# Turned probability blocks through DRAM: one write and four reads a part, in place of 16 SBUF-to-SBUF moves

## The chip, the cores and the metric

The kernel runs on one core of one Trainium2 chip. The metric is the device time of one execution in microseconds (us); the kernel before has a median of 1175.51 us over three runs.

## The reference

The inputs are `q`, `k`, `v` of shape (8, 8, 576, 64): 8 batches, 8 heads, 576 positions, 64 channels a head. All is float32.

```
q_rot, k_rot = rotate(q), rotate(k)                 # rotary embedding, per position
scores = q_rot @ k_rot^T / sqrt(64)                 # 576 x 576 for each head
attn   = exp(scores - rowmax); attn /= (rowsum + 1e-9)
x      = concat of heads of (attn @ v)              # (8, 576, 512)
x_prev = x shifted by one position, zeros first
xk, xr = mu * x + (1 - mu) * x_prev                 # two mixes, mu_k and mu_r
k = relu(xk @ w_k); v = (k * k) @ w_v               # 512 -> 1024 -> 512
out = sigmoid(xr @ w_r) * v
```

So an attention stage feeds, batch by batch, a channel mix of three matrix products.

## The kernel before, in words

**Units of work.** Heads are taken in pairs: 8 batches of 4 pairs, 32 pairs. For one pair the queries are cut into nine blocks of 128 query columns, written here as units u = 0 to 8: four from each head and a shared last one. For each unit TensorE (PE) makes 128 x 576 scores (line 417), VectorE (DVE) takes the negated row maximum `nm` (line 428), and ScalarE (ACT) writes the exponentials `pe` with their row sums (line 438). The product with `v` needs the probabilities with keys on the partitions, so they must be turned.

**Two ways of turning.** The first four pairs (`EARLY = 4`) are turned by PE through an identity matrix (`plan_turn`, line 463). The other 28 pairs are turned in two steps. First, DVE transposes 32 x 32 blocks within each group of 32 partitions (line 443) and writes them into a tile `p`, one tile for each of two parts g = 0, 1 of a pair, `[128, 18, 128]` and `[128, 18, 160]` float32. Afterwards `p` holds, on partition group a (32 partitions) and block b (one of 18 blocks of 32 keys), a block that belongs on another group of partitions. Second, `plan_move` moves it into `rows_t[g]`, `[128, 4, 5, 128 or 160]`, in which keys stand on partitions. The 18 key blocks are cut into four strips of 5, 5, 4 and 4 blocks (`STRIPS`), one for each group of 32 target partitions. One DMA takes source group a and strip s to target group s: 4 x 4 = 16 DMAs a part (lines 502 to 510), each of 32 rows. Then 20 matmuls a part make `av` (line 529), DVE multiplies by the reciprocal row sums `rb` (lines 536 and 541), and the result `xT` goes to the channel mix.

**Reciprocal sums.** For each pair, DVE inverts the sums (lines 479 to 482), one DMA writes them to a DRAM tile `inv` (line 486) and two read them back, broadcast, into `rb` (line 492). This is a way through DRAM that the kernel already has.

**Channel mix.** For each half batch (288 positions) the mixes `mxf` are split into a rounded high part and a low remainder (`mxh`, `mxl`), and each product is three matmuls of 288 columns (lines 609, 610, 611). Its weights come as 64-bit words, 20 blocks of 128 x 512, through one `raw` buffer (line 291), and DVE, ACT and POOL turn each into float32 high and low parts.

**Buffers.** One tile of each of `p` part 0, `p` part 1, `rows_t[0]`, `rows_t[1]`, one `values` tile (line 386), two tiles for loaded and rotated q and k (`nat`, line 340), one `rb`, one `raw`.

**What sets the order.** The order of instructions on every engine is written out in advance by a planner (`Plan.issue`, line 109). Each operation has a rank, a cost and its predecessors; in the planner's own model of time, an engine that comes free takes the ready operation of the lowest rank. Ranks are a pair's or half batch's start time plus offsets from the tables `R`, `EARLY_R`, `PB` and `MB` (lines 30 to 42); the `B_` numbers bias the choice of engine where there are two. All DMAs are issued by SyncE (SP). In the planner a DMA is an operation of SP with a cost of 350 ns, and then one of a single modelled DMA engine, at 360 bytes a ns, for the moves 190. On the chip each engine executes its list in that order: an SP entry whose semaphore has not come holds all entries behind it.

The changed steps stand in `dma` (line 104), and in `plan_move` (line 472), whose results `d["M", g]` the product in `plan_values` (line 543) waits for.

Of the kernel before, what the change touches and what calls it, by code (L numbers as in the profile page):

```python
# [14 lines left out]
F32 = mybir.dt.float32  # L15
# [7 lines left out]
P = 128  # L23
# [3 lines left out]
WG = (128, 160)  # L27
STRIPS = ((0, 5), (5, 5), (10, 4), (14, 4))
EARLY = 4
R = dict(k=-179.52, q=-112.39, v=-377.25, cs=587.95, mu=696.88, ld=1946.21, rope0=636.06, rope1=1296.91,  # L30
         rope2=-189.65, split0=1185.84, split1=-372.65, u0=-519.54, u1=-378.68, u2=-113.17, u3=-312.32, u4=-344.5,
         mx=-450.29, ex=-554.02, tp=586.99, dm=61.24, da=46.42, dw=-1222.76, dr2=1374.29, av=766.79, ah=73.72,
         nr=5.44, ev=-725.53, m0=154.44, mh=0.64, mk=-102.03, mr=350.75, ms=170.57, mx1=-292.97, mx2=291.49,
         mx3=-1004.93, mg=24.03, mv=17.23, dr=-272.53, key0=-863.9, key1=938.21, key2=405.18, gate0=982.35,
         gate1=-652.3, wk0=-13.84, wk1=-71.85, wr0=-294.97, wr1=132.08, wv0=-65.2, wv1=95.49)
EARLY_R = dict(k=-367.76, q=-526.32, v=-276.86, ld=-806.66, rope0=-55.23, rope1=221.54, rope2=308.84,
               split0=-128.56, split1=747.9, u0=-654.44, u1=-336.85, u2=-413.68, u3=-209.13, u4=-92.85, mx=99.4,
               ex=-456.12, tp=-58.57, dm=-427.42, da=-338.79, dw=-832.67, dr2=171.88, av=-196.14, ah=417.64,
               nr=184.01, ev=-1013.41)
PB = (-1117.66, -32.72, -757.09, -55.52, 346.01, 25.88, -122.08, -92.28)  # L40
B_COPY, B_ROPE, B_SPLIT, B_LOW, B_MIX, B_SQUARE, B_RELU = -881.07, 63.63, 520.96, 1365.24, 1028.59, -1244.85, -157.99
MB = (-73.1, -357.44, 21.16, -309.47, 391.67, -92.21, 254.91, 283.5)
CY = 12
BUFS = dict(nat=2, kh=2, kl=1, qh=2, ql=1, vs=1, pe=4, pe3=8, p0=1, p1=1, s=2, s3=3, nm=6, sums=2, rb=1, pt0=1, pt1=1, t=2, xT=5, raw=1, we=1, wm=1, mxf=2, mxh=5, mxl=5, acc=2, hr=2, kkh=8, kkl=8, rt=3)

# [5 lines left out]
def act(n):  # L51
    return 0.833 * n + 100


def dve(n):
    return 1.04 * n + 70


def dve2(n):
    return 0.52 * n + 75  # L60
# [12 lines left out]
class Plan:  # L73
# [16 lines left out]
    def op(self, engine, rank, cost, fn, after=(), uses=()):  # L90


        o = len(self.ops)
        if isinstance(engine, str):
            engine, fn = {engine: (cost, 0, engine == "G")}, lambda e, fn=fn: fn()
        opens = [s for s in uses if s.opener is None]
        for s in uses:
            s.users += 1
        for s in opens:
            s.opener = o  # L100
        self.ops.append((engine, rank, None, fn, tuple(after), tuple(uses), opens))
        return o

    def dma(self, rank, nbytes, fn, after=(), uses=(), rate=360):

        o = self.op("S", rank, 350, fn, after, uses)
        return self.op("D", rank, nbytes / rate, lambda: None, [o], uses)

    def issue(self):
# [92 lines left out]
def rope_attention_channel_mix(ctx, tc, qt, kt, v, cs, mu, w_k, w_v, w_r, out):  # L202
# [3 lines left out]
    nc = tc.nc  # L206
    B, NP, _, _, S = kt.shape
# [9 lines left out]
    dram = ctx.enter_context(tc.tile_pool(name="dram", bufs=1, space=bass.MemoryType.DRAM))  # L217
# [22 lines left out]
    def one(n, bias=0.0):  # L240

        return {"A": (act(n) + 30, 0, False), "V": (dve2(n), bias, True)}
# [6 lines left out]
    V, A, G, T = nc.vector, nc.scalar, nc.gpsimd, nc.tensor  # L249
    plan = Plan(BUFS)  # L250
    op, dma, Slot = plan.op, plan.dma, plan.slot

    def combine(e, out, a, b, op):
# [22 lines left out]
    rows_t = [const.tile([P, 4, 5, n], F32, name=f"rows_{n}") for n in WG]  # L276
# [55 lines left out]
    def plan_rope(t, d, n, src, have, plain, load_rank):  # L332
# [22 lines left out]
        def turned(which, i, t):  # L355
# [3 lines left out]
            return [o, op(two(P, B_ROPE), t, 0, lambda e: turn_last(e, which, i), [ld] + have, [slot])]  # L359

        ld = dma(load_rank, P * 8 * w, load, [], [slot])
        ms = turned("s", 1, t + d["r"]["rope0"])
        mc = turned("c", 0, t + d["r"]["rope1"])
# [11 lines left out]
    def plan_prep(t, b, g):  # L375
        d = live[b, g]
        d["r"] = EARLY_R if PAIRS.index((b, g)) < EARLY else R
        d["bg"], d["plain"] = (b, g), PAIRS.index((b, g)) < PLAIN
        first = PAIRS[0] == (b, g)
        plan_rope(t + d["r"]["k"], d, "k", kt[b, g], tables["cs"], d["plain"], -339.0 if first else t + d["r"]["k"] + d["r"]["ld"])  # L380
        plan_rope(t + d["r"]["q"], d, "q", qt[b, g], tables["cs"], d["plain"], -289.0 if first else t + d["r"]["q"] + d["r"]["ld"])
        sv = d["sv"] = Slot("vs")

        def load_v():
            d["vf"] = values_t[sv.index % BUFS["vs"]]
            nc.sync.dma_start(d["vf"], v[b, g])

        d["v"] = dma(t + d["r"]["v"] + d["r"]["ld"], P * 4 * 10 * D, load_v, [], [sv])
# [83 lines left out]
    def plan_move(t, d):  # L472


        ss, sr = d["ss"], Slot("rb")
        w = {}

        def inverse():
            V.tensor_scalar_add(d["sums"][:, 0:9], d["sums"][:, 0:9], 1e-9)
            V.reciprocal(d["sums"][:, 0:9], d["sums"][:, 0:9])  # L480
            V.tensor_copy(d["sums"][:, 9:10], d["sums"][:, 4:5])
            V.transpose(d["sums"], d["sums"])

        def write():
            w["dram"] = dram.tile([4, 32, 32], F32, tag="inv", name="inv", bufs=4)
            nc.sync.dma_start(w["dram"].rearrange("a u n -> (a u) n"), d["sums"])

        def read(x):
            if "rb" not in d:
                d["rb"] = sb.tile([P, 4, 160], F32, tag="rb", name="rb", bufs=BUFS["rb"])  # L490
            src = w["dram"][:, 5 * x:5 * x + 5, :].rearrange("a u n -> a (u n)").unsqueeze(0).to_broadcast([D, 4, 160])
            nc.sync.dma_start(d["rb"][(up, dn)[x]], src)

        o = op("V", t + d["r"]["nr"], 500, inverse, [d["E", u] for u in range(9)], [ss])
        o = dma(t + d["r"]["dw"], P * 128, write, [o], [ss])
        d["R"] = [dma(t + d["r"]["dr2"] + 0.1 * x, D * 4 * 640, lambda x=x: read(x), [o], [sr]) for x in range(2)]
        d["sr"] = sr

        if d["early"]:
            return  # L500

        def move(g, a, s):
            at, n = STRIPS[s]
            nc.sync.dma_start(rows_t[g][32 * s:32 * s + 32, a, 0:n, :], d["p", g][32 * a:32 * a + 32, at:at + n, :])  # L504

        for g, cs in enumerate(GROUPS):
            ready = [d["T", u] for c in cs for u in ((4,) if c == 4 else (c, c + 5))]
            for a in range(4):
                for s in range(4):
                    d["M", g].append(dma(t + d["r"]["dm"] + d["r"]["da"] * g + 0.01 * (4 * a + s), 32 * STRIPS[s][1] * 4 * WG[g], lambda g=g, a=a, s=s: move(g, a, s), ready, [d["sp", g], d["spt", g]], rate=190))  # L510

    N0 = S // 2

    def plan_values(t, d):
# [4 lines left out]
        for g in range(2):  # L519
# [18 lines left out]
            def divided_last(x):  # L538
                r = (up, dn)[x]
                acc = w[1][:, 0:384].rearrange("p (a n) -> p a n", a=4)[r, :, 80 - 80 * x:96 - 80 * x]  # L540
                V.tensor_tensor(out=d["x"][r, 513:S + 1].rearrange("p (a n) -> p a n", n=16), in0=acc, in1=d["rb"][r, :, 128 + 16 * x:144 + 16 * x], op=ALU.mult)

            o = op("T", t + d["r"]["av"] + d["r"]["ah"] * g, 2350 + 540 * g, products, d["M", g] + [d["v"]], [s_a, d["sv"], d["spt", g]])
            e[g] = [op("V", t + d["r"]["ev"] + d["r"]["ah"] * g, dve(256) + 30, divided, [o] + d["R"], [s_a, sx, d["sr"]])]
            if g:
                e[g] += [op("V", t + d["r"]["ev"] + d["r"]["ah"] * g + 0.1 * x, dve(64) + 30, lambda x=x: divided_last(x), [o] + d["R"], [s_a, sx, d["sr"]]) for x in range(2)]
        z = op("G", t + d["r"]["ev"], 110, lambda: G.memset(d["x"][:, 0:1], 0.0), [], [sx])
        d["X", 0], d["X", 1] = e[0] + e[1] + [z], e[0] + e[1]

    def plan_attention():  # L550
        for pi, bg in enumerate(PAIRS):
            plan.group = 2 * pi
            d, t = live[bg], PT * pi + (PB[pi] if pi < len(PB) else 0)
            plan_prep(t, *bg)
# [4 lines left out]
            for c in range(5):  # L559
                plan.group = 2 * pi + 0.1 * c  # L560
                plan_unit(t + (EARLY_R if pi < EARLY else R)[f"u{c}"], d, c)
            plan.group = 2 * pi
# [7 lines left out]
    def plan_mix(t, b, half, which, f, hold):  # L570
# [24 lines left out]
        o = op({"A": (act(n) + 130, 0, False), "V": (dve2(n) + 60, B_MIX, True)}, t, 0, previous, d["X", half] + [rest], [sx, s_f])  # L595
        o = op({"V": (dve(n) + 60, 0, True)}, t + R["mx1"], 0, mixed, [o], [sx, s_f])
        h = op(one(n, B_SPLIT), t + R["mx2"], 0, high, [o], [s_f, s_h])
# [102 lines left out]
    for b in range(B):  # L700
        plan_channel_mix(b, 4 * PT * b + R["m0"] + MB[b], 4 * PT * (b + 1) + R["m0"] + MB[b])
    with tc.manual_schedule():
# [65 lines left out]
```

## Time and profile before

| | |
|---|---|
| runs | 1166.67, 1175.51, 1175.69 us; median 1175.51 |
| profiled execution | 1166.59 us, of which the profile's span is 1164.8 us |
| PE busy | 981.5 us, 84% |
| DVE busy | 822.4 us, 71% |
| ACT, POOL busy | 532.7 us, 488.5 us |
| DMA | 157.49 MB in 95,425 packets; the SP queue's packets took 49.1% of 16 engines' span |
| HBM | 71.90 MB read, 9.96 MB written |
| PE's granted clock, mean | 0.939 of full speed |

The page first gives the busy time of each engine, then the span in slices, the DMA queues, the chain of work that ended last (followed back from the last instruction), and the costliest groups of instructions. "SPq" is SyncE issuing a DMA; "L504" is line 504. A busy share is an average over stages, so the stages are looked at by themselves in what follows: a start (to about 125 us) with the early pairs and the first weights, a stage to about 250 us in which the moves have begun and the last weights are still being made, a long even stage to about 1060 us, and a tail of channel mix alone.

### The profile page before, as it was taken

Reading aid. Unit: us, or ns where it says so; the run is one execution under the profiler, and the core shown is the slowest. Engines: PE = TensorE matmul, PEld = TensorE weight load, DVE = VectorE, ACT = ScalarE, POOL = GpSimd, SP = SyncE. Lnnn points to the kernel's source line nnn. Section 1 sums busy time; section 2 is a strip of 40 time slices with the busy share of each in tenths; the row PEclk is TensorE's granted clock in tenths of the full one; section 3 lists DMA queues with packets and bytes.
Section 4 is the critical chain, followed back from the end, with each engine's and each line's share of the span. In section 5 each row is a group of like instructions: output and inputs, shape, how many; then the busy total and the mean of one; then the engine's idle time right before and its main releaser. Section 6 shows DMA issues by size and latency. Waiting matters only on the chain.

```text
span 1164.8 us, 19561 instructions
## 1 busy us (share of the span) xinstructions
PE 981.5 (84%) x6866; PEld 791.3 (68%) x6866; DVE 822.4 (71%) x1465; ACT 532.7 (46%) x1317; POOL 488.5 (42%) x495
## 2 busy tenths in 40 slices
PE   2687688678887978999999989998988888988898
PEld 1444355466676767787778767776867776776788
DVE  6989987855775666776877777796767876663442
ACT  2556445423455344554565444555445543432133
POOL 4545357612155354436564435445445524311111
PEclk9999778579897999999999999998999998999999
DMA  5434576415564355556656556655455555443000
GB/s 171 146 120 164 160 199 176 128 51 140 138 168 113 102 150 161 137 141 182 169 155 162 152 132 192 173 152 145 140 138 158 143 135 153 119 106 79 16 22 21
DMA packets 95425, 157.49 MB, mean 135 GB/s; under 512 B 23008, under 2 KB 47584, under 8 KB 95328
## 3 DMA queue, kind: packets, MB, share of 16 engines
q1 hardware_dynamic: 95328, 156.25, 49.1%
q8 instruction: 54, 0.88, 0.3%
q14 instruction: 43, 0.35, 0.1%
HBM read 71.90 MB, written 9.96 MB: 70 GB/s over the span
## 4 chain that ended last, share of the span: by engine, by line
PE 37%; SPq 19%; DVE 18%; DMA 14%; issue 5%; POOL 3%; ACT 3%; DVEq 0%; POOLq 0%; ACTq 0%
SPq L504 17%; PE scores L609 9%; PE av L529 8%; PE scores L611 7%; PE scores L610 7%; PE scores L417 5%; DVE nm L428 4%; DMA rows<-p 4%; DVE p L443 3%; DMA xq<-in_qt 3%; DMA xk<-in_kt 2%; DMA values<-in_v 2%; DMA out_dram<-rt 1%; POOL xq L254 1%; DVE mxf L585 1%
## 5 line engine op out<-in xcount | busy, mean ns | idle before, releaser
L438 ACT ACTIVATE pe<-scores,nm 128x576 f32<-128x576 f32 x252 | 184.5, 737 | 157.4 <-DVE nm L428 141.5
L428 DVE TENSOR_REDUCE nm<-scores 128x1 f32<-128x576 f32 x288 | 204.8, 746 | 62.2 <-PE scores L417 60.8
L529 PE MATMUL av<-rows,values 128*64 128x320 f32 (+1 forms) x1280 | 185.4, 441 | 34.6 <-DMA values<-in_v 12.4
L443 DVE STREAM_TRANSPOSE p<-pe 128x576 f32<-128x576 f32 x252 | 182.9, 755 | 26.3 <-DMA rows<-p 21.1
L417 PE MATMUL scores<-kh,qh 64*128 64x288 f32 x738 | 145.0, 425 | 61.1 <-ACT pe L438 41.9
L609 PE MATMUL scores<-mxh,wk_h 128*128 128x288 f32 x496 | 157.7, 318 | 27.4 <-DVE hr L628 13.2
L609 PE MATMUL scores<-kkh,wv_h 128*128 128x288 f32 x480 | 150.9, 314 | 20.7 <-ACT rt L656 7.4
L529 PEld LDWEIGHTS av<-rows,values 128*64 128x64 f32 x1280 | 98.1, 147 | 101.5 <-issue 42.6
L254 POOL TENSOR_TENSOR mxl<-mxf,mxh 128x288 fp32r<-128x288 f32 x95 | 82.4, 871 | 196.4 <-ACT mxh L258 182.3
L417 PEld LDWEIGHTS scores<-kh,qh 64*128 64x128 f32 x738 | 82.7, 207 | 112.6 <-ACT pe L438 57.2
L610 PE MATMUL scores<-mxl,wk_h 128*128 128x288 f32 x496 | 146.3, 295 | 0.0
L611 PE MATMUL scores<-kkh,wv_l 128*128 128x288 f32 x480 | 145.0, 302 | 1.3 <-DVE wv_l L254 0.9
L611 PE MATMUL scores<-mxh,wk_l 128*128 128x288 f32 x496 | 145.8, 294 | 0.0
L610 PE MATMUL scores<-kkl,wv_h 128*128 128x288 f32 x480 | 144.5, 301 | 0.0
L609 PEld LDWEIGHTS scores<-mxh,wk_h 128*128 128x128 f32 x496 | 93.2, 188 | 53.5 <-DVE hr L628 20.1
L254 POOL TENSOR_TENSOR kkl<-hr,kkh 128x288 fp32r<-128x288 f32 x93 | 78.0, 845 | 118.4 <-ACT kkh L258 85.7
L609 PEld LDWEIGHTS scores<-kkh,wv_h 128*128 128x128 f32 x480 | 92.8, 193 | 36.3 <-ACT rt L656 11.9
L254 POOL TENSOR_TENSOR xq<-xq,turns 128x512 f32<-128x512 f32 (+1 forms) x88 | 92.8, 1073 | 50.6 <-DMA xq<-in_qt 46.2
L254 POOL TENSOR_TENSOR xk<-xk,turns 128x576 f32<-128x576 f32 x37 | 57.9, 1570 | 91.4 <-DMA xk<-in_kt 79.5
L609 PE MATMUL scores<-mxh,wr_h 128*128 128x288 f32 x248 | 82.6, 333 | 14.2 <-ACT rt L656 4.6
L611 PEld LDWEIGHTS scores<-kkh,wv_l 128*128 128x128 f32 x480 | 93.0, 194 | 2.1 <-DVE wv_l L254 1.5
L585 DVE SCALAR_TENSOR_TENSOR mxf<-xT,mu_t,mxf 128x288 f32<-128x288 f32 x128 | 85.5, 678 | 11.4 <-ACT mxf L580 10.9
(112 smaller groups left out, 1900.6 us busy)
## 6 DMA issues: line engine op xcount, KB each, us to landing
rows<-p SPq DMA_DIRECT2D x448, 80.0 KB, 2.1
rows<-p SPq DMA_DIRECT2D x224, 100.0 KB, 2.2
xq<-in_qt SPq DMA_DIRECT2D x32, 640.0 KB, 5.5
xk<-in_kt SPq DMA_DIRECT2D x32, 576.0 KB, 4.7
rows<-p SPq DMA_DIRECT2D x224, 64.0 KB, 2.0
values<-in_v SPq DMA_DIRECT2D x32, 320.0 KB, 4.5
rb<-inv SPq DMA_DIRECT2D x64, 160.0 KB, 4.0
out_dram<-rt SPq DMA_DIRECT2D x64, 144.0 KB, 2.0
```

The source lines that it names most:

```text
L254: (V if e == "V" else G).tensor_tensor(out=out, in0=a, in1=b, op=op)
L417: T.matmul(w[x][:, h, 0:H], lhsT=kind(d[q][r, c * P:(c + 1) * P]), rhs=kind(d[k][r, h * H:(h + 1) * H]), start=i == 0, stop=i == len(todo) ...
L428: V.tensor_reduce(out=w["nm", x], in_=w[x][:, :, 0:H], op=ALU.max, axis=AX.XY, negate=True)
L438: A.activation(w["p", x].rearrange("p (h n) -> p h n", h=2), w[x][:, :, 0:H], AF.Exp, bias=w["nm", x], scale=1.0, accum_out=d["sums"][:, u ...
L443: V.transpose(d["p", g][:, :, at:at + 32], w["p", x].rearrange("p (b n) -> p b n", n=32))
L504: nc.sync.dma_start(rows_t[g][32 * s:32 * s + 32, a, 0:n, :], d["p", g][32 * a:32 * a + 32, at:at + n, :])
L529: T.matmul(acc[(up, dn)[x], :, to:to + n], lhsT=d["vf"][:, 5 * x + j, :], rhs=rows_t[g][:, :, j, n * x:n * x + n], start=j == 0, stop=j == 4)
L585: V.scalar_tensor_tensor(out=x["f"], in0=d["x"][:, half * n + 1:half * n + n + 1], scalar=mu_t[:, m:m + 1], in1=x["f"], op0=ALU.mult, op1= ...
L609: T.matmul(w["a"], lhsT=w_h[:, i, sl], rhs=x["h"], start=(i == 0), stop=False)
L610: T.matmul(w["a"], lhsT=w_h[:, i, sl], rhs=x["l"], start=False, stop=False)
L611: T.matmul(w["a"], lhsT=w_l[:, i, sl], rhs=x["h"], start=False, stop=(i == count - 1))
```

## The change

For the 28 pairs that DVE turns, `plan_move` issues for each part one DMA that writes the whole tile `p` (128 rows of 18 x 128 or 18 x 160 floats) to a DRAM tile `turned0` or `turned1`, of which there are two each, and then four DMAs, one a strip, that read from DRAM what all four source groups have for that strip, straight into the 32 target partitions of `rows_t[g]`. The four reads wait for the write. The write holds `p` alone; the reads hold `rows_t[g]` alone, where each of the 16 moves held both. The reads have a new rank offset `di` behind the write's `dm`. In the planner, a DMA's cost on SP is 610 instead of 350 for all DMAs, the moves' own rate of 190 is gone, and the tables of ranks, starts and biases have other numbers throughout, so the written order of all engines is another. What is computed is the same, and nothing else in the program is changed.

```diff
-R = dict(k=-179.52, q=-112.39, v=-377.25, cs=587.95, ... ex=-554.02, tp=586.99, dm=61.24, da=46.42, ...
+R = dict(k=-170.58, q=-121.86, v=-302.6, cs=1164.53, ... ex=-799.79, tp=638.63, di=170.09, dm=471.79, da=86.98, ...
...
     def dma(self, rank, nbytes, fn, after=(), uses=(), rate=360):
 
-        o = self.op("S", rank, 350, fn, after, uses)
+        o = self.op("S", rank, 610, fn, after, uses)
         return self.op("D", rank, nbytes / rate, lambda: None, [o], uses)
...
-        def move(g, a, s):
+        def move_out(g):
+            w["p", g] = dram.tile([P, 18, WG[g]], F32, tag=f"turned{g}", name="turned", bufs=2)
+            nc.sync.dma_start(w["p", g].rearrange("p b n -> p (b n)"), d["p", g].rearrange("p b n -> p (b n)"))
+
+        def move_in(g, s):
             at, n = STRIPS[s]
-            nc.sync.dma_start(rows_t[g][32 * s:32 * s + 32, a, 0:n, :], d["p", g][32 * a:32 * a + 32, at:at + n, :])
+            src = w["p", g].rearrange("(a i) b n -> i a (b n)", a=4)[:, :, at * WG[g]:(at + n) * WG[g]]
+            nc.sync.dma_start(rows_t[g][32 * s:32 * s + 32, :, 0:n, :].rearrange("p a j n -> p a (j n)"), src)
 
         for g, cs in enumerate(GROUPS):
             ready = [d["T", u] for c in cs for u in ((4,) if c == 4 else (c, c + 5))]
-            for a in range(4):
-                for s in range(4):
-                    d["M", g].append(dma(t + d["r"]["dm"] + d["r"]["da"] * g + 0.01 * (4 * a + s), 32 * STRIPS[s][1] * 4 * WG[g], lambda g=g, a=a, s=s: move(g, a, s), ready, [d["sp", g], d["spt", g]], rate=190))
+            o = dma(t + d["r"]["dm"] + d["r"]["da"] * g, P * 18 * 4 * WG[g], lambda g=g: move_out(g), ready, [d["sp", g]])
+            for s in range(4):
+                d["M", g].append(dma(t + d["r"]["dm"] + d["r"]["da"] * g + d["r"]["di"], P * STRIPS[s][1] * 4 * WG[g], lambda g=g, s=s: move_in(g, s), [o], [d["spt", g]]))
```

More of the change, by code (lines that the diff above doesn't have):

```diff
@@ L29 @@
 EARLY = 4
[L30 to L41, printed above, removed]
@@ L42 @@
-MB = (-73.1, -357.44, 21.16, -309.47, 391.67, -92.21, 254.91, 283.5)
+R = dict(k=-170.58, q=-121.86, v=-302.6, cs=1164.53, mu=991.11, ld=1958.72, rope0=549.92, rope1=1861.93,
+         rope2=137.07, split0=1585.28, split1=-369.49, u0=-285.6, u1=-146.91, u2=-135.16, u3=-245.03, u4=-224.69,
+         mx=-295.32, ex=-799.79, tp=638.63, di=170.09, dm=471.79, da=86.98, dw=-1486.25, dr2=1804.88, av=1680.01,
+         ah=108.11, nr=-491.67, ev=-709.36, m0=142.77, mh=-13.55, mk=-153.7, mr=282.14, ms=158.17, mx1=-19.12,
+         mx2=219.25, mx3=-908.53, mg=21.82, mv=16.35, dr=-380.32, key0=-1186.84, key1=1101.65, key2=400.27,
+         gate0=1557.76, gate1=-659.69, wk0=-28.46, wk1=-245.65, wr0=-326.36, wr1=175.07, wv0=-137.55, wv1=337.66)
@@ new lines @@
+EARLY_R = dict(k=-564.0, q=-1170.11, v=-343.8, ld=-1562.58, rope0=293.9, rope1=424.08, rope2=-27.38,
+               split0=-678.82, split1=947.24, u0=48.92, u1=-764.8, u2=-518.62, u3=-170.28, u4=-518.36, mx=320.33,
+               ex=-960.19, tp=-251.82, di=-478.7, dm=-397.13, da=-510.21, dw=-405.45, dr2=471.62, av=-248.39,
+               ah=506.21, nr=448.89, ev=-1023.97)
+PB = (-1701.39, 236.47, -547.89, 58.95, 176.83, -159.49, -34.46, 8.57)
+B_COPY, B_ROPE, B_SPLIT, B_LOW, B_MIX, B_SQUARE, B_RELU = -1101.5, -35.23, 368.36, 1453.79, 1150.37, -1080.99, -375.92
@@ L43 @@
+MB = (-168.94, -271.8, -134.14, -339.86, 331.16, -643.19, 619.37, 428.48)
 CY = 12
```

## The prediction

> **What bounds the kernel now.** I read the page first (busy times, chain), then PE's waits, windows by stage, SP's timeline, and the DMA view. Page:
>
> ```profile
> span 1164.8 us, 19561 instructions
> ...
> PE 981.5 (84%) x6866; PEld 791.3 (68%) x6866; DVE 822.4 (71%) x1465; ACT 532.7 (46%) x1317; POOL 488.5 (42%) x495
> ...
> PE 37%; SPq 19%; DVE 18%; DMA 14%; issue 5%; POOL 3%; ACT 3%; DVEq 0%; POOLq 0%; ACTq 0%
> SPq L504 17%; PE scores L609 9%; PE av L529 8%; PE scores L611 7%; PE scores L610 7%; PE scores L417 5%; DVE nm L428 4%; DMA rows<-p 4%; DVE p L443 3%; DMA xq<-in_qt 3%; DMA xk<-in_kt 2%; DMA values<-in_v 2%; DMA out_dram<-rt 1%; POOL xq L254 1%; DVE mxf L585 1%
> ```
>
> PE is the busiest engine, and the issue of the moves (line 504) is the largest single entry of the chain, 17% or 198 us. That is no price. While SP issued, PE mostly had other work, so the most that any relief can give is PE's idle time, 1164.8 - 981.5 = 183 us, and only that part which a late DMA causes. PE's waits, and windows with the columns PE, PEld, DVE, ACT, POOL busy, PE clock, DMA share, GB/s:
>
> ```profile
> PE scores L417 <- ACT pe L438: 41.9, 33, 8.2
> ...
> PE av L529 <- DMA values<-in_v: 12.4, 5, 3.2
> ...
> PE av L529 <- DMA out_dram<-rt: 7.1, 2, 4.3
> PE av L529 <- DMA rows<-p: 5.6, 4, 2.1
> ...
> PE av L529 <- DMA xk<-in_kt: 3.2, 1, 3.2
> ```
>
> ```profile
> 700.00:850.00 150.00, 138.58 (x1050) 115.89 (x1049) 114.87 (x199) 75.50 (x191) 73.33 (x74) 0.98 0.59 160
> 850.00:1000.00 150.00, 126.90 (x925) 105.16 (x925) 105.16 (x188) 68.14 (x169) 67.75 (x72) 0.94 0.54 145
> ```
>
> ```profile
> 130.00:230.00 100.00, 75.35 (x354) 50.19 (x353) 82.13 (x137) 46.83 (x112) 56.80 (x50) 0.72 0.64 177
> 250.00:1000.00 750.00, 663.78 (x4928) 550.83 (x4929) 537.61 (x955) 363.90 (x910) 334.61 (x345) 0.96 0.56 148
> ```
>
> The product `av` waits for DMAs 12.4 + 7.1 + 5.6 + 3.2 = 28.3 us in all, 0.5 us for each of 56 parts. (It doesn't read the `out_dram` or `xk` transfers; a release put down to them must be a move or a value load that landed beside them.) From 250 us on PE is 88.5% busy; its best 150 us are at 92.4%, its worst here at 84.6%. The stage from 130 to 230 us is different: PE is at 75%, its clock at 0.72, DVE at 82%.
>
> **SP's work, the part removed.** The moves by the line's own view, and SP's timeline (start, us, what, count):
>
> ```profile
> L504 SPq DMA_DIRECT2D rows<-p x896: 507/589/1989, 125.9 to 1057.3; - x180
> ```
>
> ```profile
> 537.29 10.06 SPq L504 DMA_DIRECT2D rows<-p  x16
> ...
> 646.66 21.65 SPq L504 DMA_DIRECT2D rows<-p  x32
> 668.41 1.29 SPq L492 DMA_DIRECT2D rb<-inv  x2
> 669.75 0.60 SPq L386 DMA_DIRECT2D values<-in_v  x1
> ```
>
> A part takes 10.06 us, so a move's pitch is 10.06 / 16 = 0.63 us (589 ns and a gap), and 896 of them hold SP for 564 us of the 932 us in which they occur. The change leaves 56 x 5 = 280 DMAs. An issue with many rows is not dearer here: the value load's 128 rows took 0.60 us. So 280 x 0.63 = 176 us are left, and 388 us of SP are freed, 13.9 us a pair. The planner counted 350 ns for an issue, so a part was planned at 5.6 us and took 10.06; 610 is close to the measured pitch.
>
> What this gives is in four places. **First**, PE's 28.3 us of waits at `av`. The timeline above shows the typical one: 32 moves in a row, and the value load stands behind them. With 10 issues a pair that queue falls from 21.65 us to 6.3. What is late next is PE itself or the read back, so I don't count it all: 20 us saved (ends 0 and 28.3).
>
> **Second**, the stage from 130 to 230 us. SP's timeline, and the chain there in order of time:
>
> ```profile
> 172.92 10.97 SPq L504 DMA_DIRECT2D rows<-p  x16
> 183.93 1.29 SPq L492 DMA_DIRECT2D rb<-inv  x2
> 185.32 0.55 SPq L291 DMA_DIRECT2D raw<-in_w_r  x1
> ```
>
> ```profile
> 185.32 6.08 DMA raw<-in_w_r
> ```
>
> The weight block's load is issued only after 16 moves and two reads, and its landing is then on the chain. SP is full in this stage; with two parts ahead of a load, 2 x (16 - 5) x 0.63 = 14 us fewer bring it forward. But DVE, which converts the weights, has only 100 - 82.1 = 17.9 us idle. So the gain lies between 0 and 17.9 us; I take 12, nearer to the upper end because the moves and the loads behind them take most of the chain there.
>
> **Third**, the single `p` tile, and the moves' wait for the rows:
>
> ```profile
> DVE p L443 <- DMA rows<-p: 21.1, 15, 3.4
> ```
>
> ```profile
> SPq L504 <- PE av L529: 35.2, 13, 8.4
> ```
>
> Before, `p` stayed taken until the last of 16 moves, and these could not begin before the previous `av` had released the rows. Now one write releases it. DVE's 21.1 us may go, but it has 750 - 538 = 212 us idle from 250 us on, so I count 3 us (ends 0 and 21). The 35.2 us wait of SP goes over to the reads; behind it stand q, k and value loads as before.
>
> **Fourth**, the new order of all engines. The trace can't show it. Its bounds are the stages: if 250 to 1000 us ran like its best window, 663.78 / 0.924 = 718 us, 32 us less; like its worst, 663.78 / 0.846 = 785 us, 35 us more. An order made with the true issue cost should meet fewer unplanned waits; I take 8 us less, a quarter of the good end.
>
> **What is added.** DMA issues (KB each, us to landing), and the queue's packets, MB and share in three windows: 15 us with moves alone, the last 99 us with DRAM writes alone, the first 14 us with loads alone:
>
> ```profile
> rows<-p SPq DMA_DIRECT2D x448, 80.0 KB, 2.1
> rows<-p SPq DMA_DIRECT2D x224, 100.0 KB, 2.2
> xq<-in_qt SPq DMA_DIRECT2D x32, 640.0 KB, 5.5
> ...
> rows<-p SPq DMA_DIRECT2D x224, 64.0 KB, 2.0
> values<-in_v SPq DMA_DIRECT2D x32, 320.0 KB, 4.5
> ...
> out_dram<-rt SPq DMA_DIRECT2D x64, 144.0 KB, 2.0
> ```
>
> ```profile
> q1 hardware_dynamic: 1036, 1.82, 51.8%
> ```
>
> ```profile
> q1 hardware_dynamic: 1728, 1.77, 5.1%
> ```
>
> ```profile
> q1 hardware_dynamic: 1132, 3.22, 68.4%
> ```
>
> *Transfer time.* The moves carry 448 x 80 + 224 x 100 + 224 x 64 KB = 74.3 MB. Moving between SBUF partitions runs at 1.82 MB / (15 x 0.518 us) = 234 GB/s of full engines, DRAM writes at 1.77 / (99 x 0.051) = 351, loads at 3.22 / (14 x 0.684) = 336. So 318 us of all 16 engines become 74.3/0.351 + 74.3/0.336 = 433 us. That is 115 us more in 932, and the DMA share of 0.56 becomes 0.68. Were both ways as slow as the moves, it would be 636 us and 0.90. I take 0.68, since these are the nearest kinds of transfer. Loads then land somewhat later: the value load's 4.5 us grows by a fifth, 0.9 us. I count a third of that for 28 pairs, 8 us lost (ends 0 and 25).
>
> *Latency from the last transpose to the rows.* Before: 15 x 0.63 + 2.1 = 11.5 us, if SP is free. After: the write of 1.18 MB (part 1: 1.47) costs, from the 2.0 us of the 147 KB output, 2.0 + 1.03/0.351 = 4.9 us (5.8), or, from the loaded row of `xq`, 5.5 + 0.52/0.336 = 7.1 us (7.9). The last of four reads is issued 1.9 us later and lands like a value load, 4.5 us: 6.4 in all. Together 11.3 to 14.3 us, between nothing and 2.8 us more. The queue ahead of a part is 15 us shorter where two parts come together, so I price the difference at nothing in the forecast; it returns as the rival below.
>
> The Trainium skill speaks against this step: "DMA: Bandwidth & Descriptors", section "Anatomy of one DMA", puts a fixed cost of about 2 us on a DMA, mostly the receipt of the last write, and says that HBM is the heaviest target. By its figures the write would be an estimated 2.0 + 1.18/0.436 = 4.7 us. The trace doesn't show a heavier receipt: 147 KB to DRAM landed in 2.0 us, 82 KB within SBUF in 2.1.
>
> **Sum**: -20 - 12 - 3 - 8 + 8 = -35 us on the profiled execution's 1166.6 (span 1164.8 and 1.8 around it): 1131.6. Of the three timed runs one is at that time and two are 9 us above it; with half of that, 4.5 us, I predict 1136 us as the median.
>
> **The rivals.** *No change* (0.19). SP's share of the chain was time in which PE was busy; the gain falls where scores wait for exponentials (41.9 us, the largest of PE's waits) and DVE. Only the waits marked `rows` and half of the stage at 130 to 230 us go, 5.6 + 6, and the transfers give 8 back: 1175.5 - 4 = 1172.
>
> *Slower: two landings in series* (0.19). The write's landing holds the SP queue, and the read's follows. If each landing is 1 us later than planned, at a DMA share above 0.68, each `av` comes 2 us late, and PE executes in order. Half of that for 56 parts is 56 us; with 31 us of the gains kept, 1175.5 + 56 - 31 = about 1200. It decides when `av` waits more than 0.5 + 35/56 = 1.1 us a part in place of 0.5. For it: the value load already takes 4.5 us, and the chain has 14% of DMA. Against it: the planner allows for the write's time, and PE has channel-mix work to put between.
>
> *Much faster: the stage's clock* (0.10).
>
> ```profile
> 130.00:255.00 125.00, 92.89 (x440) 64.85 (x440) 98.04 (x165) 54.51 (x129) 64.12 (x57) 0.72 0.53 149
> ```
>
> PE worked 92.9 us here at 0.72 of full clock. At the 0.98 of the best window the same work takes 68 us, 25 us less. If SP's relief fills PE's gaps in this stage, that comes on top of 18 us there, and the order gives its good end of 32: 1166.6 - 25 - 18 - 32 = 1092. That idle time lowers the clock is the rule of the Trainium skill, "TensorE: Matmul & The Clock Gate", section "Part 1: The HAM clock gate (the "warmup" mystery)"; the trace agrees in so far as 0.72 stands beside 75% busy and 0.98 beside 92%.
>
> **How the numbers follow.** The forecast has 0.52 (1105 to 1163), no change 0.19 (1164 to 1187), slower 0.19 (1188 to 1225), much faster 0.10 (1090 to 1105). A measurement of this kernel tells about 1% from no change, so faster means under 1163.8 us: 0.62; within 1%: 0.19; slower: 0.19. The range 1098 to 1192 leaves out half of the much faster case and three quarters of the slower one, 0.05 + 0.14. The forecast's own range is 1105 to 1163.
>
> **What would show it.** Right: the moves' issue falls to about 176 us of SP, PE's waits at `av` for DMAs fall under 10 us, DVE's waits for `p` vanish, DMA share near 0.68 with the write landing in 5 to 8 us, and weights are done before 230 us with a higher clock. Wrong: `av` waits for the reads above 60 us in all, the write landing over 8 us, SP idle on the write with loads behind it, or the DMA share near 0.9.

## The result, and the profile after

The changed kernel takes 1092.08 us (median, 1088.76 to 1097.0), against 1175.6 us of the kernel before beside it: a ratio of 0.930, with a 95% interval from 0.925 to 0.936. That is 83 us faster. I had forecast 1136 us, so the direction was right and the gain about twice what I said; the time lies 6 us below my range. It is the number of the "much faster" rival, but not by that rival's mechanism, as is shown below.

The page after, to be read against the one before: span, busy times, the SP queue's packets, and the chain.

```profile
span 1088.6 us, 18700 instructions
...
PE 958.2 (88%) x6866; PEld 778.6 (72%) x6866; DVE 816.1 (75%) x1419; ACT 551.0 (51%) x1356; POOL 498.9 (46%) x502
...
q1 hardware_dynamic: 92640, 230.53, 75.2%
...
PE 60%; DMA 20%; DVE 13%; ACT 3%; issue 3%; POOL 1%; SPq 1%; DVEq 0%; ACTq 0%; POOLq 0%
PE scores L614 14%; PE av L534 12%; PE scores L616 11%; PE scores L615 11%; PE scores L417 9%; DMA rows<-turned 8%; DVE nm L428 2%; DVE p L443 2%; DMA rb<-inv 2%; DMA values<-in_v 2%; DMA out_dram<-rt 2%; DMA xk<-in_kt 2%; DMA turned<-p 2%; PE turn L463 1%; DMA xq<-in_qt 1%
```

SP's share of the chain fell from 19% to 1%. PE's share rose from 37% to 60%. DMA's share rose too, from 14% to 20%: the reads have 8% and the writes 2%, where the moves' transfers had 4%. The DMA queue, at 49.1% before, is now at 75.2% of a shorter span. PE's idle time went from 183.3 to 130.4 us, 52.9 us less, and its busy time from 981.5 to 958.2, 23.3 us less, at a clock of 0.953 in place of 0.939. Together these are the 76 us between the two spans.

Of PE's waits, first the kernel before, then the changed kernel (line, releaser, us in total, times, longest). Lines 609 and 529 before are 614 and 534 after.

```profile
PE scores L609 <- ACT hr L626: 16.7, 27, 1.6
PE scores L609 <- DVE hr L628: 16.0, 27, 2.3
PE scores L609 <- DVE rt L665: 12.5, 18, 3.2
...
PE scores L609 <- ACT rt L656: 11.9, 19, 2.0
```

```profile
PE scores L417 <- ACT pe L438: 29.6, 14, 7.7
...
PE scores L614 <- ACT rt L661: 10.5, 21, 1.0
PE scores L614 <- ACT hr L631: 9.3, 14, 2.6
PE scores L614 <- DVE rt L670: 7.6, 11, 2.5
...
PE av L534 <- DMA rows<-turned: 4.5, 4, 1.4
PE av L534 <- DMA rb<-inv: 4.2, 1, 4.2
...
PE scores L614 <- DVE hr L633: 4.1, 11, 1.1
...
PE av L534 <- DMA values<-in_v: 3.8, 2, 2.7
```

The waits of `av` for DMAs fell from 28.3 to 12.5 us. But the channel mix's waits for `hr` and `rt`, in which no DMA is named, fell more, from 57.1 to 31.5, and the scores' wait for exponentials from 41.9 to 29.6. These three account for 53.7 us, as much as the idle time that went.

SP's own waits show the same from the other side. Before, then after:

```profile
SPq L666 <- DVE rt L665: 119.8, 20, 27.5
...
SPq L340 <- POOL kl L254: 31.6, 9, 10.5
SPq L486 <- DVE sums L482: 28.2, 19, 4.2
...
SPq L386 <- PE av L529: 11.6, 4, 9.0
```

```profile
SPq L671 <- DVE rt L670: 167.8, 40, 27.5
...
SPq L340 <- POOL kl L254: 77.5, 17, 9.6
SPq L386 <- PE av L534: 59.6, 23, 5.2
SPq L486 <- DVE sums L482: 56.3, 29, 12.6
```

After, SP waits at its loads and stores for what the engines must do first, that is, it is early. Before, it came to the same entries later and waited less at them. Summed over all rows of this view between 130 and 950 us, SP waited 209 of 820 us before and 566 after.

The issues and landings of the new DMAs, by the two lines' own views and the DMA view:

```profile
L504 SPq DMA_DIRECT2D turned<-p x56: 319/337/555, 126.1 to 933.1; - x56
```

```profile
L509 SPq DMA_DIRECT2D rows<-turned x224: 302/430/1662, 132.4 to 968.7; - x112
```

```profile
turned<-p SPq DMA_DIRECT2D x28, 1440.0 KB, 8.1
rows<-turned SPq DMA_DIRECT2D x112, 320.0 KB, 9.8
turned<-p SPq DMA_DIRECT2D x28, 1152.0 KB, 6.8
rows<-turned SPq DMA_DIRECT2D x56, 400.0 KB, 8.8
```

An issue takes 0.34 us (write) or 0.43 (read) in the median, less than a move's 0.59. By the medians 56 x 0.34 + 224 x 0.43 = 115 us go into all of them, where 896 x 0.59 = 529 us went into the moves (564 with the gaps between them). Some reads' issues took up to 1.66 us, so the 115 is an estimate from below. I had forecast 176.

### The profile page after: what moved, and what is told of

Its sections match the earlier page's. It is cut to its first block, busy times and chain, and to the rows that moved or that the text cites. A ratio compares the mean times of both kernels' runs of the same rounds, so it can differ in the third digit from the quotient of the medians.

```text
span 1088.6 us, 18700 instructions
## 1 busy us (share of the span) xinstructions
PE 958.2 (88%) x6866; PEld 778.6 (72%) x6866; DVE 816.1 (75%) x1419; ACT 551.0 (51%) x1356; POOL 498.9 (46%) x502
## 3 DMA queue, kind: packets, MB, share of 16 engines
q1 hardware_dynamic: 92640, 230.53, 75.2%
## 4 chain that ended last, share of the span: by engine, by line
PE 60%; DMA 20%; DVE 13%; ACT 3%; issue 3%; POOL 1%; SPq 1%; DVEq 0%; ACTq 0%; POOLq 0%
PE scores L614 14%; PE av L534 12%; PE scores L616 11%; PE scores L615 11%; PE scores L417 9%; DMA rows<-turned 8%; DVE nm L428 2%; DVE p L443 2%; DMA rb<-inv 2%; DMA values<-in_v 2%; DMA out_dram<-rt 2%; DMA xk<-in_kt 2%; DMA turned<-p 2%; PE turn L463 1%; DMA xq<-in_qt 1%
## 5 line engine op out<-in xcount | busy, mean ns | idle before, releaser
L443 DVE STREAM_TRANSPOSE p<-pe 128x576 f32<-128x576 f32 x252 | 186.3, 760 | 10.5 <-ACT pe L438 10.1
L534 PE MATMUL av<-rows,values 128*64 128x320 f32 (+1 forms) x1280 | 175.3, 423 | 20.4 <-issue 5.2
L417 PE MATMUL scores<-kh,qh 64*128 64x288 f32 x738 | 145.3, 428 | 48.8 <-ACT pe L438 29.6
L254 POOL TENSOR_TENSOR mxl<-mxf,mxh 128x288 fp32r<-128x288 f32 x90 | 78.7, 876 | 173.0 <-ACT mxh L258 143.3
L534 PEld LDWEIGHTS av<-rows,values 128*64 128x64 f32 x1280 | 91.8, 141 | 83.9 <-issue 31.0
L417 PEld LDWEIGHTS scores<-kh,qh 64*128 64x128 f32 x738 | 81.7, 207 | 98.0 <-ACT pe L438 41.9
L254 POOL TENSOR_TENSOR kkl<-hr,kkh 128x288 fp32r<-128x288 f32 x101 | 90.0, 902 | 90.2 <-ACT kkh L258 67.8
L254 POOL TENSOR_TENSOR xk<-xk,turns 128x576 f32<-128x576 f32 x46 | 70.9, 1553 | 91.4 <-DMA xk<-in_kt 73.7
L254 POOL TENSOR_TENSOR xq<-xq,turns 128x128 f32<-128x128 f32 (+1 forms) x96 | 98.9, 1048 | 17.5 <-DMA xq<-in_qt 17.5
L590 DVE SCALAR_TENSOR_TENSOR mxf<-xT,mu_t,mxf 128x288 f32<-128x288 f32 x128 | 90.1, 718 | 10.7 <-ACT mxf L585 10.0
L615 PEld LDWEIGHTS scores<-mxl,wk_h 128*128 128x128 f32 x496 | 94.0, 189 | 1.5 <-POOL mxl L254 1.3
L616 PEld LDWEIGHTS scores<-mxh,wk_l 128*128 128x128 f32 x496 | 93.8, 189 | 0.2 <-POOL wk_l L254 0.2
```

The costliest lines, as they stand in the source:

```text
L254: (V if e == "V" else G).tensor_tensor(out=out, in0=a, in1=b, op=op)
L417: T.matmul(w[x][:, h, 0:H], lhsT=kind(d[q][r, c * P:(c + 1) * P]), rhs=kind(d[k][r, h * H:(h + 1) * H]), start=i == 0, stop=i == len(todo) ...
L443: V.transpose(d["p", g][:, :, at:at + 32], w["p", x].rearrange("p (b n) -> p b n", n=32))
L534: T.matmul(acc[(up, dn)[x], :, to:to + n], lhsT=d["vf"][:, 5 * x + j, :], rhs=rows_t[g][:, :, j, n * x:n * x + n], start=j == 0, stop=j == 4)
L590: V.scalar_tensor_tensor(out=x["f"], in0=d["x"][:, half * n + 1:half * n + n + 1], scalar=mu_t[:, m:m + 1], in1=x["f"], op0=ALU.mult, op1= ...
L615: T.matmul(w["a"], lhsT=w_h[:, i, sl], rhs=x["l"], start=False, stop=False)
```

## The experiments

**Theory 1**: SP's issue time set the pace. **Theory 2**: the new written order is the gain. **Theory 3**: the gain is that the write holds only `p` and the reads only the rows. **Theory 4**, added after the second run: what that run gained was DMA transfer time. A median of the kernel before, run beside them, is given for each group.

### SP's time put back, and taken away (kernel before: 1172.29 us)

One run puts issue time back into the changed kernel's order:

```diff
-            nc.sync.dma_start(rows_t[g][32 * s:32 * s + 32, :, 0:n, :].rearrange("p a j n -> p a (j n)"), src)
+            for a in range(4):
+                nc.sync.dma_start(rows_t[g][32 * s:32 * s + 32, a, 0:n, :].rearrange("p j n -> p (j n)"), src[:, a, :])
```

> The changed kernel with its written order kept on all engines, but each of a part's four reads from DRAM is issued as four reads, one for each source group: one write and 16 reads a part, the same bytes by the same way. Only SP's issue time comes back: 12 more issues a part at 0.45 to 0.63 us, 5.4 to 7.6 us a part, 300 to 420 us of SP in all. Theory 1 (SP's issue time was the limit): most of the gain goes, 1150 us or more. Theory 2 (the new order of all engines is the gain) and theory 3 (the gain is that the write holds only p and the reads hold only the rows): the time stays below 1110 us.

Measured: 1165.76 us, a ratio of 0.996 (0.992 to 0.999) to the kernel before. That is 74 us above the changed kernel. Nearly all of the gain is gone, though the order, the bytes, the way and the buffers are those of the changed kernel. PE's waits in this run:

```profile
PE scores L417 <- ACT pe L438: 38.3, 21, 8.8
PE scores L615 <- DVE rt L671: 20.0, 12, 6.3
...
PE scores L615 <- ACT hr L632: 17.0, 15, 5.3
PE scores L615 <- ACT rt L662: 12.2, 23, 1.2
...
PE scores L615 <- DVE hr L634: 7.7, 11, 3.8
```

The mix's four sum to 56.9 us, as much as the 57.1 of the kernel before, where the changed kernel had 31.5. So these waits come and go with SP's issues, in one and the same order. SP's timeline in this run:

```profile
499.64 10.59 SPq L510 DMA_DIRECT2D rows<-turned  x16
510.33 0.37 SPq L386 DMA_DIRECT2D values<-in_v  x1
510.75 7.39 SPq L510 DMA_DIRECT2D rows<-turned  x16
```

Again a value load stands between two blocks of 16 issues, as in the kernel before. Theories 2 and 3 by themselves can't explain this run, which has their order and their holds without the gain.

The next takes issue time away in the order of the kernel before:

```diff
-            nc.sync.dma_start(rows_t[g][32 * s:32 * s + 32, a, 0:n, :], d["p", g][32 * a:32 * a + 32, at:at + n, :])
+            if a == 3:
+                nc.sync.dma_start(rows_t[g][:, s, 0:n, :], d["p", g][:, at:at + n, :])
```

> The kernel before with its written order kept on all engines, but a part's 16 moves are four, each of 128 rows, one a strip, from each partition of p to the same partition of the rows: the same bytes within SBUF, no way through DRAM, 12 issues a part fewer. The blocks thus come to the wrong partitions, so the products are of other numbers; their work is the same. Theory 1 (SP's issue time): 1095 to 1125 us, as SP gets back some 12 x 0.63 = 7.6 us a part without the DRAM trip. Theory 2 (order): 1160 us or more. Theory 3 (separate holds of p and rows): 1160 us or more, since every move still holds both.

Measured: 1066.4 us, 0.909 (0.903 to 0.916). It is 106 us faster in the old order, with every move still holding `p` and rows, and without DRAM; that is more than Theory 1 expected, 1095 to 1125 us. The 250 to 850 us stage (PE, PEld, DVE, ACT, POOL busy, clock, DMA share, GB/s), of the kernel before, of this run, and of the changed kernel:

```profile
250.00:850.00 600.00, 536.88 (x4006) 445.67 (x4006) 432.44 (x768) 295.76 (x742) 266.86 (x274) 0.97 0.56 148
```

```profile
250.00:850.00 600.00, 572.10 (x4433) 478.22 (x4435) 489.16 (x849) 331.38 (x831) 301.33 (x310) 1.00 0.49 167
```

```profile
250.00:850.00 600.00, 567.06 (x4367) 479.01 (x4367) 477.31 (x809) 336.39 (x840) 313.04 (x315) 0.98 0.91 253
```

PE is busy 89% before and 95% in both others; all engines rise together, which fits a queue that feeds them all. PE's waits in this run:

```profile
PE scores L417 <- ACT pe L438: 22.0, 14, 4.0
...
PE scores L610 <- ACT hr L627: 12.8, 25, 0.8
PE scores L610 <- DVE hr L629: 11.9, 21, 1.0
PE scores L610 <- ACT rt L657: 9.5, 18, 1.1
PE scores L610 <- DVE rt L666: 8.3, 14, 1.0
```

The wait for exponentials fell by 19.9 us, the mix's by 14.6 to 42.5, and no wait of `av` for a DMA is left (28.3 before). PE's idle time went from 183.3 to 115.4 us and its busy time from 981.5 to 948.6, at a clock of 0.966.

### DRAM in the old order (kernel before: 1172.29 us)

```diff
-            nc.sync.dma_start(rows_t[g][32 * s:32 * s + 32, a, 0:n, :], d["p", g][32 * a:32 * a + 32, at:at + n, :])
+            if a == s == 0:
+                w["p", g] = dram.tile([P, 18, WG[g]], F32, tag=f"turned{g}", name="turned", bufs=2)
+                nc.sync.dma_start(w["p", g].rearrange("p b n -> p (b n)"), d["p", g].rearrange("p b n -> p (b n)"))
+            if a == 3:
+                src = w["p", g].rearrange("(a i) b n -> i a (b n)", a=4)[:, :, at * WG[g]:(at + n) * WG[g]]
+                nc.sync.dma_start(rows_t[g][32 * s:32 * s + 32, :, 0:n, :].rearrange("p a j n -> p a (j n)"), src)
```

> The kernel before with its written order kept on all engines, but in the place of a part's first move stands the write to DRAM, and in the place of its last four moves the four reads; the other 11 are left out. SP issues less, but it stands still between the write and the first read until the write has landed (5 to 8 us), with all loads behind it. Theory 1: SP is held for about 0.6 + 7 + 2 = 9.6 us a part against 10.1 before, so little changes, 1150 to 1185 us. Theory 2 (order): the same, 1160 to 1190. Only if the way through DRAM were a gain by itself would it come below 1130.

Measured: 1190.13 us, 1.013 (1.007 to 1.019), 1.3% slower than before and just above both expected ranges. SP's longest wait says why:

```profile
SPq L509 <- DMA turned<-p: 379.5, 53, 11.6
```

SP stood at the first read for the write's landing, 7 us at each of 53 times, with the loads behind it. This is the mechanism of my slower rival. In the old order, with nothing put between write and read, nothing is left of a gain; in the changed kernel this wait is 11.1 us in 7 times.

### What the bytes cost (kernel before: 1172.29 and 1172.73 us)

```diff
-            nc.sync.dma_start(w["p", g].rearrange("p b n -> p (b n)"), d["p", g].rearrange("p b n -> p (b n)"))
+            nc.sync.dma_start(w["p", g].rearrange("p b n -> p (b n)")[:, 0:9 * WG[g]], d["p", g].rearrange("p b n -> p (b n)")[:, 0:9 * WG[g]])
...
-            src = w["p", g].rearrange("(a i) b n -> i a (b n)", a=4)[:, :, at * WG[g]:(at + n) * WG[g]]
-            nc.sync.dma_start(rows_t[g][32 * s:32 * s + 32, :, 0:n, :].rearrange("p a j n -> p a (j n)"), src)
+            src = w["p", g].rearrange("(a i) b n -> i a (b n)", a=4)[:, :, at * WG[g] // 2:(at + n) * WG[g] // 2]
+            nc.sync.dma_start(rows_t[g][32 * s:32 * s + 32, :, 0:n, :].rearrange("p a j n -> p a (j n)")[:, :, 0:n * WG[g] // 2], src)
```

> The changed kernel in its written order, with half of the bytes: the write takes the first half of each row of p, and each read half of its strip. The rest of the rows tile keeps old numbers, so half of the probabilities are left out; all engines' work and SP's issues are the same. If the extra transfers cost time on the path (the DMA share is 0.92 to 0.97 from 400 to 850 us), the time falls to 1070 to 1085 us; by my estimate of 8 us for the loads that land later, about 1084. If transfers lie beside other work, it stays at 1088 to 1096.

Measured: 1049.3 us, 0.895 (0.890 to 0.900), 43 us below the changed kernel, and more than the 1070 to 1085 us that I expected if transfers cost time. So the transfers do stand on the path at a share of 0.91. With the bytes the landings got shorter too: a strip's read went from 9.8 to 4.8 us, a value load from 6.3 to 3.7, and DMA's share of the chain from 20% to 2%. How much comes from the late loads and how much from the ways' own landings was not separated. The SP queue's packets here:

```profile
q1 hardware_dynamic: 92640, 156.21, 51.5%
```

These 156.21 MB are as many bytes as the kernel before moves, 156.25.

The same halving in the kernel before:

```diff
-            nc.sync.dma_start(rows_t[g][32 * s:32 * s + 32, a, 0:n, :], d["p", g][32 * a:32 * a + 32, at:at + n, :])
+            nc.sync.dma_start(rows_t[g][32 * s:32 * s + 32, a, 0:n, 0:WG[g] // 2], d["p", g][32 * a:32 * a + 32, at:at + n, 0:WG[g] // 2])
```

> The kernel before with its 16 moves a part and its written order, each move with half of every row (half of the queries' probabilities are not moved): DMA bytes of the moves halved, SP's issues the same. Theory 1 (SP's issue time is the limit): 1155 to 1176 us, nearly no change. Theory 4 (what the four-move run gained was DMA transfer time, not SP's time): 1100 us or less.

Measured: 1176.55 us, 1.004 (1.001 to 1.008), no gain at all:

```profile
q1 hardware_dynamic: 195680, 119.09, 38.1%
```

```profile
L504 SPq DMA_DIRECT2D rows<-p x896: 585/602/2310, 123.7 to 1066.8; - x180
```

The engines' DMA share fell from 49% to 38%, an issue still took 0.60 us, and the time stayed. This removes Theory 4: in the kernel before, the number of moves counted and their bytes did not.

### How the cost of issues sets in (kernel before: 1172.73 us)

```diff
-            nc.sync.dma_start(rows_t[g][32 * s:32 * s + 32, :, 0:n, :].rearrange("p a j n -> p a (j n)"), src)
+            for a in (0, 2):
+                nc.sync.dma_start(rows_t[g][32 * s:32 * s + 32, a:a + 2, 0:n, :].rearrange("p a j n -> p a (j n)"), src[:, a:a + 2, :])
```

> The changed kernel in its written order with eight reads a part in place of four, each of two source groups: 4 more issues a part at 0.45 us. Theory 1, with 12 more issues having cost 74 us: if the cost is even, 1092 + 25 = 1117 us; if it sets in only as SP becomes full, less than 1105. Theories 2 and 3: 1092 as in the changed kernel.

Measured: 1095.61 us, 0.933 (0.929 to 0.938). Four more issues cost 3.5 us, which the noise does not tell from nothing; twelve cost 74. SP's waits between 130 and 950 us sum to 566 us with four reads, 475 with eight, 281 with sixteen. So here the queue's issues cost little while it has room to wait, and much once it has not.

### The written order (kernel before: 1172.73, 1176.78 and 1169.11 us)

The 16 moves, with the changed kernel's tables (`R` to `MB`) and issue cost, so that this line of the planner is the changed kernel's:

```diff
-        o = self.op("S", rank, 350, fn, after, uses)
+        o = self.op("S", rank, 610, fn, after, uses)
```

> The 16 moves of the kernel before, planned with the tables of the changed kernel and its SP cost of 610. Theory 1 (SP's issue time): no gain, 1165 to 1210 us. Theory 2 (tables and true issue cost are the gain): 1120 us or less.

Measured: 1197.06 us, 1.020 (1.016 to 1.024). Without SP's relief the new tables are no gain, but a loss of 24 us.

The changed kernel's write and reads, with the old tables and an issue cost of 350 (one line of the tables is shown):

```diff
...
-         mx=-295.32, ex=-799.79, tp=638.63, di=170.09, dm=471.79, da=86.98, dw=-1486.25, dr2=1804.88, av=1680.01,
+         mx=-450.29, ex=-554.02, tp=586.99, di=0.0, dm=61.24, da=46.42, dw=-1222.76, dr2=1374.29, av=766.79, ah=73.72,
...
-        o = self.op("S", rank, 610, fn, after, uses)
+        o = self.op("S", rank, 350, fn, after, uses)
```

> The change's write and four reads, but planned with the tables of the kernel before and its SP cost of 350 (di = 0): all queues are ordered anew by the planner, with numbers that were never chosen for this way. Theory 1 (SP's issue time): most of the gain is there, 1095 to 1130 us. Theory 2 (the new tables are the gain): 1160 us or more.

Measured: 1151.91 us, 0.982 (0.977 to 0.987). This missed both expectations. So the new ways need an order that fits them. With half of the bytes as well, by the edit shown above:

> The change's write and reads planned with the tables of the kernel before (the run of 1152 us), with half of the bytes; half of the probabilities are not moved. If what that run lost against the changed kernel is transfer time (DMA share 0.87 to 0.97), it falls to 1060 to 1085 us. If it is the order that the old tables give, it gains no more than the changed kernel did, 43 us: 1105 to 1115 or more.

Measured: 1096.76 us, 0.933 (0.928 to 0.937), between the two expected ranges: 55 us come from the bytes, and 47 us stay between it and the changed kernel with half bytes. Two more runs separate the planner's issue cost from the tables; each has one of the two edits just shown, the old tables alone or the 350 alone:

> The change's write and reads, the tables of the kernel before, and SP's cost of 610 in the planner (the run of 1152 us had the same tables and 350). If the true issue cost is what makes the order fit: 1100 to 1125 us. If it is the ranks in the tables: within 15 us of 1152.

> The changed kernel with SP's cost of 350 in the planner in place of 610, its tables kept. If the issue cost makes the order fit: 1115 to 1150 us. If it is the ranks: within 15 us of 1092.

Measured: 1148.98 us, 0.980 (0.974 to 0.986), and 1126.98 us, 0.965 (0.961 to 0.969). All with the write and four reads:

| | issue cost 350 | issue cost 610 |
|---|---|---|
| old tables | 1151.91 | 1148.98 |
| new tables | 1126.98 | 1092.08 |

The cost alone does nothing that the noise would show for the old tables (3 us) and 35 us for the new; the tables give 25 or 57. The numbers belong together, so that neither share stands by itself. What in the old tables' order loses is not settled. The trace of the run of 1151.91 us shows SP with room, 606 us of waits between 130 and 950 us, and PE waiting for the mix:

```profile
PE scores L614 <- DVE hr L633: 22.3, 27, 4.3
PE scores L614 <- DVE rt L670: 21.2, 20, 3.1
```

These were 4.1 and 7.6 us in the changed kernel; which rank causes it was not tried. The run with the new tables and 350 is alike: SP waits 599 us, and the mix's four waits sum to 53.9. So room in SP's list was needed for the gain, but was not enough for it.

### Looking for a better version (kernel before: 1172.79 and 1176.78 us)

Two mixtures of the changed kernel send one part by the 16 moves (`move` as before) and the other through DRAM. The first is shown; its twin has `g == 1`.

```diff
+            if g == 0:
+                for a in range(4):
+                    for s in range(4):
+                        d["M", g].append(dma(t + d["r"]["dm"] + d["r"]["da"] * g + 0.01 * (4 * a + s), 32 * STRIPS[s][1] * 4 * WG[g], lambda g=g, a=a, s=s: move(g, a, s), ready, [d["sp", g], d["spt", g]], rate=190))
+                continue
```

> A mixture for a better version: the changed kernel's tables and part 1 through DRAM, but part 0 by the 16 moves within SBUF. SP issues 21 times for a pair in place of 10 (32 before); part 0's bytes go once over the DMA engines instead of twice, so their share falls from about 0.95 to about 0.75 in the even stage. If issue time costs in proportion to what is put back, and transfers too: 1092 + 50 - 19 = about 1120 us. If SP's cost sets in only near its limit: 1065 to 1085, better than both kernels.

> The other mixture: part 0 through DRAM and part 1 by the 16 moves. The same issues as its twin, a little less on the DMA engines (part 1 is the larger). By the same two cases: about 1118 us, or 1065 to 1085.

Measured: 1117.36 us, 0.954 (0.950 to 0.959), and 1102.46 us, 0.943 (0.939 to 0.947). Both have fewer bytes and more issues than the changed kernel, and neither beats it. SP's waits between 130 and 950 us sum to 362 and 372 us.

The last lays the DRAM tile out as the rows tile: eight writes, two reads.

```diff
-            w["p", g] = dram.tile([P, 18, WG[g]], F32, tag=f"turned{g}", name="turned", bufs=2)
-            nc.sync.dma_start(w["p", g].rearrange("p b n -> p (b n)"), d["p", g].rearrange("p b n -> p (b n)"))
+            w["p", g] = dram.tile([P, 4, 5, WG[g]], F32, tag=f"turned{g}", name="turned", bufs=2)
+            for a in range(4):
+                for h, m in ((0, 5), (1, 4)):
+                    dst = w["p", g][64 * h:64 * h + 64, a, 0:m, :].rearrange("(s i) j n -> i s (j n)", s=2)
+                    nc.sync.dma_start(dst, d["p", g][32 * a:32 * a + 32, 10 * h:10 * h + 2 * m, :].rearrange("p (s j) n -> p s (j n)", s=2))
...
-            at, n = STRIPS[s]
-            src = w["p", g].rearrange("(a i) b n -> i a (b n)", a=4)[:, :, at * WG[g]:(at + n) * WG[g]]
-            nc.sync.dma_start(rows_t[g][32 * s:32 * s + 32, :, 0:n, :].rearrange("p a j n -> p a (j n)"), src)
+            if s % 2:
+                return
+            m, r = (5 if s == 0 else 4), slice(32 * s, 32 * s + 64)
+            nc.sync.dma_start(rows_t[g][r, :, 0:m, :].rearrange("p a j n -> p a (j n)"), w["p", g][r, :, 0:m, :].rearrange("p a j n -> p a (j n)"))
```

> For a better version: the changed kernel in its written order, with the DRAM tile laid out as the rows tile. The write is eight DMAs, one for each source group and half of the strips, and the read two, each of 64 target partitions in place of 32 with runs of up to 10 KB. Five more issues a part: eight reads cost 3 us for four more. If reads into 64 partitions make better use of the DMA engines, their share falls under 0.9 and the time to 1070 to 1085 us; if the bytes alone set the share, 1092 to 1105.

Measured: 1138.9 us, 0.967 (0.960 to 0.973), worse than either expectation.

```profile
400.00:850.00 450.00, 411.24 (x3144) 348.69 (x3142) 340.50 (x580) 244.85 (x612) 225.99 (x231) 0.97 0.95 243
```

The DMA share stayed at 0.95, so longer runs and more target partitions did not make the transfers cheaper. Where the added 47 us come from was not separated. SP's waits fell to 408 us of 820, and the waits of `av` for DMAs rose from 12.5 to 28.4; this points at the eight writes that stand ahead of the reads, but does not show it. No run of the reference's whole work beat the changed kernel.

## Why the prediction was right or wrong

**"That is no price": the step that failed.** I set aside SP's 17% of the chain, took PE's idle time as the most that SP's relief could give, and priced the relief by PE's waits for DMAs, 28.3 us at `av`. That term itself was well sized: 20 forecast, 15.8 measured. But it was the wrong measure. Twelve of sixteen issues taken away were worth 106 us in the old order, and twelve put back cost 74 in the new one. With them moved waits that name no DMA: in the changed kernel's order, with the issues put back, the mix's waits rose from 31.5 to 56.9 us and the scores' from 29.6 to 38.3. By which steps a late entry of SP reaches these waits was not followed. PE's busy time moved too, which a bound by idle time leaves out. Between 130 and 970 us SP's waits in the trace of before sum to 218 of 840 us; the other 622 are issues and the gaps between them. I had quoted the 564 us of the moves' issue and read them as work beside PE.

**The stage at 130 to 230 us, 12 us: wrong.** PE's busy time there went from 75.4 to 74.1 us.

```profile
130.00:230.00 100.00, 74.13 (x355) 49.83 (x356) 84.27 (x140) 48.30 (x115) 60.11 (x52) 0.77 0.99 292
```

The last weight load was issued at 236 us, before at 232. So the weights did not come sooner. In the four-move run, with a DMA share of 0.53 in this stage, it was issued at 221 us; in the changed kernel with half of the bytes, with 0.69, at 227. This fits a relief of SP of about the forecast size, 11 us, that the share of 0.99 took back. The gain is in the later stages: the moves' span shrank from 932 us to 843 (line 504's first issue at 126.1, line 509's last at 968.7), 89 us less; what follows the last of them grew from 107 us to 120.

**"Much faster" by the clock: the number, not the mechanism.** The clock from 125 to 250 us went from 0.71 to 0.73 only. The clock's part over the whole span is small: 981.5 us at 0.939 would be an estimated 967 at 0.953, 14 us of the 76. The best window as a ceiling, 92.4% busy, was wrong too: from 550 to 700 us the changed kernel's PE is busy 148.3 of 150 us.

**`p` and rows, 3 us.** DVE's 21.1 us of waits for `p` are gone, as forecast. They are gone in the four-move run as well, which kept both holds and gained more than the change, so the separate holds are not needed for it.

**The new order, 8 us: wrong as a separate term.** It is a loss of 24 us without the relief, and with it the tables are a gain of 25 or 57. My bound of 32 was read from the best window of a kernel that SP paced.

**The transfers, 8 us: much too small.** The two ways cost an estimated 819 - (572 - 318) = 565 us of full DMA engines (819 is 75.2% of the span, 572 is 49.1% of the one before; all other transfers are taken to cost what they did), not 433: 148.6 MB at 263 GB/s, where I took 351 and 336 from windows in which either went alone. The run with half of the bytes agrees: 819 - 539 = 280 us for the other half. So the share came to 0.91, just above my upper bound of 0.90, and half of the bytes cost 43 us. I had priced only the value load. This error and the first ran against each other, so that the forecast came out nearer than its terms were.

**Latency, priced at nothing.** The writes landed in 6.8 and 8.1 us, near my loaded bound of 7.1 and 7.9; a read took about 9 where I had 4.5. The Trainium skill's figures, "DMA: Bandwidth & Descriptors", section "Anatomy of one DMA — SWDGE (gpsimd) path", had given an estimated 4.7 us for the first write, too little here; they are fitted to DMAs that GpSimd issues, and these are SP's. `av` waited only 4.5 us for the rows, since the order puts other work between write and read. But the reads' 8% and the writes' 2% of the chain show that the latency was not nothing. The run with DRAM in the old order shows the price without that cover.

The range failed on the side of the gain: its low end stood on a rival of the wrong kind, with 0.10, while the likeliest cause of a large gain, a saturated SP, had no case of its own. Two of the signs that I had named for "wrong" came true beside this gain, a DMA share near 0.9 and a write that lands after more than 8 us.

## What to carry to other kernels

Look at an issuing queue as at any in-order engine: see how much of its time goes into issues and how much is left as waits. Here a queue that waited 209 of 820 us paced the kernel, whatever the compute engines' own waits named, and at 475 us of waits its issues no longer showed. Room in the queue is not enough by itself, as the runs with the old tables show. A fuller test is to take issues away with as little other change as can be, here 1172 to 1066 us, and to put them back. When fewer, larger DMAs are bought with a second trip, put other work between the two halves in the written order, and price the extra bytes at the rate that a loaded trace shows, here 263 GB/s and not the 336 to 351 of a single kind alone.

## What was not expected of the hardware

A DMA's issue is not the same for all: in the median, moves within SBUF of 32 rows took 0.59 us of SP, a write of 128 rows to DRAM 0.34, and a read from DRAM 0.43. The moves of 128 rows took 0.60 and the sixteen reads a part 0.42, so neither the rows nor the number in a row makes the difference; what does is open, as the load of `xk` from DRAM took 0.59 as well. The Trainium skill, "DMA: Bandwidth & Descriptors", section "Issuing engines are not separate DMA queues", says that the time to initiate a DMA is usually small relative to the DMA itself. Here it was 0.63 us a move against 2.1 us to landing, and it paced the kernel.

Moves within SBUF ran at 234 GB/s of full DMA engines with 32 rows, by the window in the prediction. With 128 rows, from a partition to itself, the whole queue of the four-move run took 43.0% of 1064 us, 457 us; less the 254 us of all other transfers, the same estimate as above, that is 203 us for 74.3 MB, 366 GB/s. Whether the rows or the unchanged partition does it, these runs don't tell apart.
